# Attention and maxout feed-forward: the feed-forward matmuls cut into 64x64 tiles, in pairs of row halves, with single score units among them

## The chip, the cores and the metric

One core of a Trainium2 chip. The time is device microseconds of one execution; the figure for a kernel is the median of its runs. Profile lines give microseconds from the span's start, and "ns" where they say so. TensorE (PE; its weight loads are PEld), VectorE (DVE), ScalarE (ACT), GpSimd (POOL) and SyncE (SP, which only issues transfers here) each work through their own instruction list in order and wait for one another by semaphores.

## The reference

```python
# q, k, v: 8 batches, 12 heads, 448 positions, 64 wide
scores = scale * np.matmul(q, k.transpose(0, 1, 3, 2))
m = np.max(scores, axis=-1, keepdims=True)
e = np.exp(scores - m)
attn = e / (np.sum(e, axis=-1, keepdims=True) + np.exp(-m) + 1e-09)
x = np.matmul(attn, v)              # then (batch, position, head * 64): 3584 x 768
h = np.maximum(np.maximum(x @ w1, x @ w2), x @ w3)      # w1, w2, w3: 768 x 768
out = h @ w_out                                         # w_out: 768 x 768, out 3584 x 768
```

## The kernel before, in words

Everything that TensorE reads is half precision; PSUM sums are single precision. The order of all work is written out by hand: each engine runs its instructions in the order in which the kernel's functions issue them.

**Attention.** Four heads of a batch form a group, so there are 24 groups, three to a batch (`groups`). For each group k, q and v are loaded by GpSimd's queue (`load_group`, L103) and q and k are transposed. For groups 1 to 6 TensorE does that (`pe_transpose_both`, L172, up to the constant `PE_TR` = 7, L542), 28 transposes and two VectorE copies a group; from group 7 on VectorE reorders q and k (`copy_qk`, L158) and SyncE's queue issues a transposing DMA (`dma_transpose`, L212). Scores are made in *units*: seven key blocks `j` of 64 keys, each four 64x64 matmuls of 448 columns, one on each quarter of the array (`score_tile`, L228; `TILES`, L221, gives row half `r` and column half `c`). The matmuls of row half `r` write PSUM bank `r` of a pair of banks. ScalarE takes the exponential of a unit (L253), VectorE sums the units (`sum_e`, L257). When a group's units are done, `den_group` (L283) makes the column sums of the exponentials with four 64x64 matmuls, and ScalarE turns them into reciprocals by a logarithm and an exponential (`recip_group`, L298); `av_group` (L305) multiplies the exponentials with v, 28 64x64 matmuls into two banks, and VectorE writes the products with the reciprocals into `xT` of the batch (L321).

**Feed-forward.** It is cut into *pieces*. An up piece (`up_piece`, L425) makes 128 hidden features by 448 tokens for one of the three weights: six full 128x128 matmuls of 448 columns into one bank, which VectorE copies or maximizes into `hT`. There are 18 for a batch. (`up_part`, L443, is a smaller form for the first batch.) An output piece (`out_piece`, L469) makes 128 tokens by 384 output features: six full matmuls of 384 columns; VectorE scales the result into `o_sb`, and SyncE's queue writes it out. There are 6 for a batch of even number and 8 for one of odd number (`add_out`).

**The order around the change.** Groups 0 to 3 follow a list of operations (`start`, L566 and on). From group 4 on a loop goes over *visits*: three score units in a row, in some visits with the transposes of a later group, the `av` of one group and the `den` of the next; between two visits `moe` (L526) takes pieces from a list until it has spent a given number of columns (`gap`), and after each piece it issues one waiting VectorE sum (`jobs`). So TensorE goes from full tiles to 64x64 tiles and back once for each visit. When a batch's third `av` is done, its pieces are added to the list.

**PSUM.** Eight banks: two single ones (`single`), taken in turn by pieces and `av`, and three pairs (`double`), taken in turn by score units, `den` and the pieces next to wide visits.

Of the kernel before, what the change touches and what calls it, by code (L numbers as in the profile page):

```python
# [10 lines left out]
FP32 = mybir.dt.float32  # L11
# [11 lines left out]
def kernel(  # L23
# [40 lines left out]
    small = ctx.enter_context(tc.tile_pool(name="small", bufs=2))  # L64
    xt_pool = ctx.enter_context(tc.tile_pool(name="xt", bufs=2))
    ht_pool = ctx.enter_context(tc.tile_pool(name="ht", bufs=2))
    out_pool = ctx.enter_context(tc.tile_pool(name="outp", bufs=3))


    ps1 = ctx.enter_context(tc.tile_pool(name="ps1", bufs=2, space=bass.MemoryType.PSUM))  # L70
    ps2 = ctx.enter_context(tc.tile_pool(name="ps2", bufs=1, space=bass.MemoryType.PSUM))
    turn = [0]

    ctx.enter_context(tc.manual_schedule())

# [3 lines left out]

    def double(name, shape=(512,), dtype=FP32):  # L80
        turn[0] += 1
        return ps2.tile([128, 2, *shape], dtype, tag=f"pair{turn[0] % 3}", name=name)

    groups = [(b, g) for b in range(B) for g in range(NG)]
    raw = {}
# [72 lines left out]
    def copy_qk(i, n):  # L158
# [4 lines left out]
            out=st["qk16"][:, n].rearrange("p j s d -> p s j d"), in_=raw[i]["kq"[n]]  # L163
        )

    def transpose_slots(out, src):
        for s in range(2):
            nc.tensor.transpose(
                out=out[s * KC : s * KC + KC], in_=src[:, s], identity=ident16
            )  # L170

    def pe_transpose_both(i, in_pair=0):  # L172
        st = state.setdefault(i, {})
        st["qkT"] = att_pool.tile([128, 2, NJ, 128], MMDT, tag="qkT", name="qkT")
        if in_pair:
            pair = double("trT", (8, 128), MMDT)
            trT = [pair[:, n, 0:NJ] for n in range(2)]
        else:
            trT = [single("trT", (NJ, 128), MMDT) for n in range(2)]
        for n in range(2):  # L180
            for j in range(NJ):
                transpose_slots(trT[n][:, j, :], raw[i]["kq"[n]][:, :, j])
        for n in range(2):
            nc.vector.tensor_copy(
                out=st["qkT"][:, n].rearrange("p j c -> p (j c)"),
                in_=trT[n].rearrange("p j c -> p (j c)"),
            )


    def first_group():  # L190
# [27 lines left out]
        )  # L218


    TILES = ((0, 0), (0, 1), (1, 0), (1, 1))  # L221
    QK_HALF = {(0, 0): 0, (0, 1): 1, (1, 0): 1, (1, 1): 0}
    V_SLOT = {(0, 0): 0, (0, 1): 1, (1, 0): 1, (1, 1): 0}

    def half(n):
        return slice(n * KC, n * KC + KC)

    def score_tile(qkT, out, j, q0, q1):  # L228
        for r, c in TILES:
# [72 lines left out]
            out=st["rb"], in_=st.pop("lnd"), func=AF.Exp, bias=math.log(LAMBDA), scale=-1.0  # L302
        )

    def av_group(i):  # L305
        b, g = groups[i]
        st = state.pop(i)
        eT, v16 = st["eT"], raw[i].pop("v")
        if g == 0:
            new_x(b)  # L310
        banks = [single("av") for _ in range(2)]
        for j in range(NJ):
            av_tiles(
                [t[:, 0:S] for t in banks],
                lambda r, c: v16[half(r), V_SLOT[r, c], j],
                lambda r, c: eT[half(r), j, c],
                j == 0,
                j == NJ - 1,
            )
        for r in range(2):  # L320
            nc.vector.tensor_tensor(  # L321
                out=xT[b][:, 2 * g + r, :], in0=banks[r][:, 0:S], in1=st["rb"][:, r], op=ALU.mult
            )


    PARTS = ((0, 3), (3, NJ))
# [95 lines left out]
    hT = {}  # L422
    outs = {}

    def up_piece(b, fc, i, bank=None):  # L425
        if b % 2 == 0 and fc == 0 and i == 0:
            hT[b // 2] = ht_pool.tile([128, NFC, 2 * S], MMDT, tag="hT", name="hT")
        dst = hT[b // 2][:, fc, (b % 2) * S : (b % 2) * S + S]
        p_i = single("p_i") if bank is None else bank
        for dc in range(NDC):  # L430
            nc.tensor.matmul(  # L431
                out=p_i[:, 0:S],
                lhsT=w_sb[i][:, dc, ts(fc, 128)],
                rhs=xT[b][:, dc, :],
                start=(dc == 0),
                stop=(dc == NDC - 1),
            )
        if i == 0:
            nc.vector.tensor_copy(out=dst, in_=p_i[:, 0:S])  # L439
        else:  # L440
            nc.vector.tensor_tensor(out=dst, in0=dst, in1=p_i[:, 0:S], op=ALU.max)  # L441
# [24 lines left out]
    NW = DM // NH  # L466
    NT = 2 * S // 128

    def out_piece(bp, t, nh, bank=None):  # L469
        if nh == 0:  # L470
            outs[0] = out_pool.tile([128, DM], FP32, tag="o_sb", name="o_sb")
        o_sb = outs[0]
        op_ps = single("op_ps") if bank is None else bank
        for fc in range(NFC):
            nc.tensor.matmul(  # L475
                out=op_ps[:, 0:NW],
                lhsT=hT[bp][:, fc, ts(t, 128)],
                rhs=wout_sb[:, fc, ts(nh, NW)],
                start=(fc == 0),
                stop=(fc == NFC - 1),  # L480
            )
        last = bp == B // 2 - 1 and t == NT - 1
        cut = nh * NW + (NW // 2 if last and nh == NH - 1 else NW)
        nc.vector.tensor_scalar(  # L484
            out=o_sb[:, nh * NW : cut],
            in0=op_ps[:, 0 : cut - nh * NW],
            scalar1=1.0 / LAMBDA,
            scalar2=None,
            op0=ALU.mult,
        )  # L490
        if cut < nh * NW + NW:
            nc.scalar.activation(  # L492
                out=o_sb[:, cut:DM], in_=op_ps[:, NW // 2 : NW], func=AF.Copy, scale=1.0 / LAMBDA
            )
        if last or nh == NH - 1:
            cols = ts(nh, NW) if last else slice(0, DM)
            for n in range(2):
                b, j = divmod(2 * t + n, NJ)
                b += 2 * bp
                rows = out[b * S : (b + 1) * S].rearrange("(p j) m -> j p m", j=NJ)  # L500
                eng = nc.scalar if last and n == 1 else nc.sync
                eng.dma_start(out=rows[j][:, cols], in_=o_sb[half(n), cols])

    pieces = []

    def add_out(b):
        for t in range(0, 3) if b % 2 == 0 else range(3, 7):
            for nh in range(NH):
                pieces.append((out_piece, (b // 2, t, nh), NFC * (NW + 6)))

    def add_pieces(b):
        for fc in range(NFC):
            for i in range(3):
                pieces.append((up_piece, (b, fc, i), NDC * (S + 6)))
        add_out(b)

    credit = [0.0]
    jobs = []

    def flush():  # L520
        while jobs:
            f, a = jobs.pop(0)
            f(*a)


    def moe(cols, first_in_pair=False, last_in_pair=False):  # L526
# [7 lines left out]
        for n, (f, a, w) in enumerate(run):  # L534
            in_pair = (first_in_pair and n == 0) or (last_in_pair and n == len(run) - 1)
            f(*a, bank=double("piece")[:, 0] if in_pair else None)
            if jobs:
                f, a = jobs.pop(0)
                f(*a)

    NI = len(groups)
    PE_TR = 7  # L542

    load_weight(0, 0, 256)
    load_weight(0, 256, DFF)
# [8 lines left out]
        load_group(i, "v")  # L554
        load_group(i + 1, "kq")

    def add_parts(b, i, part):
        for fp in range(NFC // 2):
            pieces.append((up_part, (b, fp, i, part), 1.0))

    for i, part in ((0, 0), (1, 0), (0, 1), (1, 1), (2, 0), (2, 1)):
        add_parts(0, i, part)
    def sums(i, *units):
        for j in units:
            jobs.append((sum_e, (i, j)))
# [18 lines left out]
    """  # L584
    for op in start.split():
        ops[op[0]](*(int(n) for n in op[1:]))
    credit[0] = 0.0
    for i in range(NG):
        state.pop(i)
    pieces[:] = [  # L590
        (f, a, 2 * NDC * ((PARTS[a[3]][1] - PARTS[a[3]][0]) * KC + 6)) for f, a, w in pieces
    ]
    add_out(0)

    units = [(i, j) for i in range(NG + 1, NI) for j in range(NJ)]
    visits = []
    done = NG
    while units or done < NI:  # L600
        now, units = units[:3], units[3:]
        turned = [i + 1 for i, j in now if j == 3 and i + 1 < PE_TR]
        num = None
        if len(visits) >= 1 and (not turned or done == NG) and (not now or done < now[0][0]):
            num = done
            done += 1
        visits.append((now, turned, num))
    visits.append(([], [], NI))

    gap = sum(w for f, a, w in pieces) / 7.5  # L610
    for n, (now, turned, num) in enumerate(visits):
        for i, j in now:
            if j == 0:
                if i + 2 < NI:
                    load_group(i + 2, "v")
                if i + 3 < NI:
                    load_group(i + 3, "kq")
        wide = num is not None or bool(turned)
        visit(now[:2] if wide else now)
        for i in turned:  # L620
            pe_transpose_both(i)
        if num is not None:
            if num > NG:
                b, g = groups[num - 1]
                av_group(num - 1)
                if g == NG - 1:
                    add_pieces(b)
                    gap = sum(w for f, a, w in pieces) / 7
        if wide:
            visit(now[2:])  # L630
        if num is not None:
            if num < NI:
                den_group(num)
                recip_group(num)
        for i, j in now:
            if j > 0:
                sums(i, j)
            if j == 4 and PE_TR <= i + 2 < NI:
                for n_ in range(2):
                    copy_qk(i + 2, n_)  # L640
                dma_transpose(i + 2)
        last = n == len(visits) - 1
        wide_next = not last and bool(visits[n + 1][1] or visits[n + 1][2] is not None)
        moe(float("inf") if last else gap, wide, wide_next)
        flush()


# [28 lines left out]
```

## Time and profile before

| | before |
|---|---|
| median of 13 runs | 333.74 us (332.55 to 338.3) |
| the profiled execution | 335.65 us |
| its span, first to last instruction | 333.8 us |
| granted TensorE clock, mean | 0.993 |
| TensorE matmuls | 3,281, busy 318.7 us |
| VectorE busy | 236.4 us (71%) |
| ScalarE busy | 188.4 us (56%) |
| DMA traffic | 41.47 MB, mean 124 GB/s |

The span is one execution under the profiler; the runs behind the median are others. The chain of waits that ended last gives TensorE 76% of the span, DMA 15% and the rest to the others; the DMA share lies in the first 65 us. Matmuls overlap in the pipeline, so the mean duration of one (353 ns for 448 columns) is longer than the distance from one start to the next, and only the latter tells the pace.

### The profile page before, as it was taken

What the parts mean: (1) busy time and instruction counts of PE and PEld (TensorE: products, weight loads), DVE (VectorE), ACT (ScalarE), POOL (GpSimd) and SP (SyncE); (2) the same over time, 40 slices, a digit from 0 to 9 for tenths busy, and PEclk for the clock granted to TensorE, in tenths of its full rate; (3) what the DMA queues carried; (4) which work ended last, traced back from release to release, by engine and by line L of the source; (5) the groups of instructions that cost most, each with busy time, mean ns of one, the idle gap of its engine ahead of it and who ended that gap; (6) DMA issues with size and microseconds to landing.
All of it is one profiled execution on the core that took longest, in us unless ns stands there. A gap on an engine that the chain in (4) does not pass through costs nothing.

```text
span 333.8 us, 7919 instructions
## 1 busy us (share of the span) xinstructions
PE 318.7 (95%) x3281; PEld 174.8 (52%) x3281; DVE 236.4 (71%) x443; ACT 188.4 (56%) x227; POOL 101.0 (30%) x172
## 2 busy tenths in 40 slices
PE   6779999899999999999999999999999999999994
PEld 5657676444445545454445545454445545455552
DVE  3446579698877787787868787787878776865552
ACT  2599568697476566666476566657475566410000
POOL 8857549854044041244044032244010000000000
PEclk9799999999999999999999999999999999999999
DMA  8999999999778991989577992989550800013006
GB/s 143 157 190 206 200 193 174 167 205 241 93 82 98 221 188 21 136 137 204 80 90 90 189 197 45 133 150 195 80 84 2 215 32 0 2 47 96 0 11 177
DMA packets 62179, 41.47 MB, mean 124 GB/s; under 512 B 34624, under 2 KB 58688, under 8 KB 62144
## 3 DMA queue, kind: packets, MB, share of 16 engines
q0 software_dynamic: 26208, 21.70, 45.5%
q1 hardware_dynamic: 35632, 18.85, 28.7%
q8 instruction: 25, 0.41, 0.5%
q10 hardware_dynamic: 304, 0.43, 0.5%
q14 instruction: 10, 0.08, 0.1%
HBM read 43.84 MB, written 11.01 MB: 164 GB/s over the span
## 4 chain that ended last, share of the span: by engine, by line
PE 76%; DMA 15%; POOL 3%; DVE 2%; issue 2%; ACT 1%; DVEq 0%; POOLq 0%
PE p_i L431 33%; PE op_ps L475 13%; PE piece L431 11%; PE stp L231 8%; PE av L275 8%; DMA w<-in_moe_w_dram 7%; DMA ld_q<-in_q_dram 3%; DMA w<-in_moe_w_out_dram 3%; PE piece L475 2%; DMA ld_k<-in_k_dram 1%; DVE eS L261 1%; PE den L275 1%; POOL ld_v L98 1%; POOL ld_k L98 1%; POOL ld_q L98 1%
## 5 line engine op out<-in xcount | busy, mean ns | idle before, releaser
L253 ACT ACTIVATE eT<-stp 128x896 f16<-128x896 f32 x147 | 126.2, 916 | 88.5 <-PE stp L231 88.4
L431 PE MATMUL p_i<-xT,w 128*128 128x448 f16 x576 | 114.7, 353 | 0.0
L431 PEld LDWEIGHTS <-w 128*128 128x128 f16 x756 | 71.0, 98 | 75.2 <-issue 12.7
L98 POOL DMA_DIRECT2D ld_v<-in_v_dram x50 | 30.5, 618 | 130.0 <-PE stp L231 125.5
L261 DVE TENSOR_TENSOR eS<-eS,eT 128x896 f16<-128x896 f16 x105 | 64.8, 617 | 0.8
L441 DVE TENSOR_TENSOR hT<-hT,p_i 128x448 f16<-128x448 f16 x69 | 42.9, 621 | 16.7 <-PE p_i L431 16.7
L231 PE MATMUL stp<-qkT 64*64 64x448 f16 (+2 forms) x756 | 49.8, 340 | 3.4 <-DVE hT L463 1.9
L475 PE MATMUL op_ps<-w,hT 128*128 128x384 f16 x270 | 46.9, 327 | 0.0
L475 PEld LDWEIGHTS <-hT 128*128 128x128 f16 x336 | 31.6, 98 | 25.3 <-issue 3.2
L321 DVE TENSOR_TENSOR xT<-av,rb 128x448 f16<-128x448 f32 x42 | 24.3, 619 | 21.5 <-PE av L275 21.5
L431 PE MATMUL piece<-xT,w 128*128 128x448 f16 x180 | 39.1, 353 | 0.0
L98 POOL DMA_DIRECT2D ld_q<-in_q_dram x50 | 30.7, 635 | 6.5 <-DMA w<-in_moe_w_out_dram 1.9
L231 PEld LDWEIGHTS <-qkT 64*64 64x64 f16 x756 | 18.0, 107 | 25.8 <-issue 21.3
L275 PE MATMUL av<-eT,ld_v 64*64 64x448 f16 x588 | 31.5, 349 | 0.0
L484 DVE TENSOR_SCALAR o_sb<-op_ps 128x384 f32<-128x384 f32 (+1 forms) x45 | 24.7, 548 | 7.8 <-PE op_ps L475 7.8
L98 POOL DMA_DIRECT2D ld_k<-in_k_dram x48 | 29.1, 622 | 1.2 <-DMA w<-in_moe_w_dram 1.1
L275 PEld LDWEIGHTS <-ld_v 64*64 64x64 f16 x756 | 21.4, 107 | 11.4 <-issue 1.4
L439 DVE CAST hT<-p_i 128x448 f16<-128x448 f32 x27 | 16.8, 624 | 10.3 <-PE p_i L431 10.3
L340 ACT ACTIVATE eTp<-stp 128x768 f16<-128x768 f32 (+3 forms) x24 | 18.0, 819 | 9.0 <-PE stp L231 9.0
L452 PEld LDWEIGHTS <-w 128*128 128x128 f16 x216 | 18.6, 98 | 5.0 <-issue 3.3
L294 ACT ACTIVATE lnd<-den 128x896 f32<-128x896 f32 x21 | 19.2, 913 | 3.6 <-PE den L275 3.6
L492 ACT ACTIVATE o_sb<-op_ps 128x192 f32<-128x192 f32 x1 | 0.3, 330 | 36.7 <-DVE o_sb L484 36.7
(48 smaller groups left out, 204.7 us busy)
## 6 DMA issues: line engine op xcount, KB each, us to landing
out_dram<-o_sb SPq DMA_DIRECT2D x54, 192.0 KB, 3.1
ld_q<-in_q_dram POOLq DMA_DIRECT2D x50, 112.0 KB, 5.4
ld_v<-in_v_dram POOLq DMA_DIRECT2D x50, 112.0 KB, 4.4
ld_k<-in_k_dram POOLq DMA_DIRECT2D x48, 112.0 KB, 4.9
w<-in_moe_w_dram POOLq DMA_DIRECT2D x6, 192.0 KB, 8.1
w<-in_moe_w_out_dram POOLq DMA_DIRECT2D x3, 384.0 KB, 7.6
w<-in_moe_w_dram POOLq DMA_DIRECT2D x2, 384.0 KB, 7.8
w<-in_moe_w_dram POOLq DMA_DIRECT2D x1, 576.0 KB, 8.9
```

The costliest lines, as they stand in the source:

```text
L98: eng.dma_start(out=dst[hp * KC : hp * KC + KC].rearrange("p s j d -> p s (j d)"), in_=src[:, half_heads(name, hp)],)
L231: nc.tensor.matmul(out=out[half(c), r], lhsT=qkT[half(r), 0, j, h], rhs=qkT[half(r), 1, q0:q1, h], start=True, stop=True,)
L253: nc.scalar.activation(out=st["eT"][:, j], in_=stp[:, :, 0:S], func=AF.Exp, scale=scale, bias=-math.log(EDIV))
L261: nc.vector.tensor_tensor(out=st["eS"], in0=st["eT"][:, 0] if j == 1 else st["eS"], in1=st["eT"][:, j], op=ALU.add,)
L275: nc.tensor.matmul(out=outs[r][half(c)], lhsT=weights(r, c), rhs=moving(r, c), start=start, stop=stop,)
L294: nc.scalar.activation(out=st["lnd"], in_=dps[:, :, 0:S], func=AF.Ln, bias=1.0 / EDIV)
L321: nc.vector.tensor_tensor(out=xT[b][:, 2 * g + r, :], in0=banks[r][:, 0:S], in1=st["rb"][:, r], op=ALU.mult)
L431: nc.tensor.matmul(out=p_i[:, 0:S], lhsT=w_sb[i][:, dc, ts(fc, 128)], rhs=xT[b][:, dc, :], start=(dc == 0), stop=(dc == NDC - 1),)
L441: nc.vector.tensor_tensor(out=dst, in0=dst, in1=p_i[:, 0:S], op=ALU.max)
L452: nc.tensor.matmul(out=p_i[:, ts(j, nq)], lhsT=w_sb[i][:, dc, ts(2 * fp + j, 128)], rhs=xT[b][:, dc, q0 * KC : q1 * KC], start=(dc == 0), ...
L475: nc.tensor.matmul(out=op_ps[:, 0:NW], lhsT=hT[bp][:, fc, ts(t, 128)], rhs=wout_sb[:, fc, ts(nh, NW)], start=(fc == 0), stop=(fc == NFC - 1),)
L484: nc.vector.tensor_scalar(out=o_sb[:, nh * NW : cut], in0=op_ps[:, 0 : cut - nh * NW], scalar1=1.0 / LAMBDA, scalar2=None, op0=ALU.mult,)
```

## The change

The part up to group 6 stays as it is except for three things: `PE_TR` becomes 8, so group 7 too is transposed on TensorE; the transposes of groups 4 to 7 are cut into 64x64 tiles (`transpose_tiles`, 56 small ones a group instead of 28 of 128x64); and two output pieces of the first batch are held back for later.

From group 7, unit 3, on there are no visits. The third pair of PSUM banks is given up, and two single banks take its place, so four single banks turn among the pieces (`ring_bank`) and two pairs among scores, `den` and `av`. A feed-forward piece of six steps is cut twice: each 128x128 matmul becomes four 64x64 ones (row half by column half), and the two row halves of a piece run at different times. A *step* issues the two lower-row matmuls (`r` = 0) of one piece and then the two upper-row matmuls (`r` = 1) of an earlier piece, which trails by `LAG` = 8 half steps and adds to what the lower half left in its bank. An upper half begins with an instruction that waits until the piece's last lower matmuls are done (`wait_for`). Where the next lower half belongs to an output piece, and an up piece of the same hidden block is still in work, the lower half is left out of a step (`idle`).

Score units, `den` and `av` are put singly among the steps, by a table of weights for each group (`ORDER`). `rate` spreads the steps that are left over the three groups of a batch. VectorE's sums and products are issued a given number of steps later (`after`). The last two output pieces of a batch are held until the next batch's up pieces have been listed (`held`). `up_piece` and `out_piece` get a flag, with which they issue the evacuation alone. The output buffers become four.

The core of the diff:

```diff
-    out_pool = ctx.enter_context(tc.tile_pool(name="outp", bufs=3))
+    out_pool = ctx.enter_context(tc.tile_pool(name="outp", bufs=4))
...
+    def transpose_tiles(outs, src):
+        for r, c in TILES:
             nc.tensor.transpose(
-                out=out[s * KC : s * KC + KC], in_=src[:, s], identity=ident16
+                out=outs[r][half(c)], in_=src[half(r), c], identity=ident16[half(r), half(r)]
             )
...
-    PE_TR = 7
+    PE_TR = 8
...
+    HELD = 2
+    held = pieces[-HELD:]
+    del pieces[-HELD:]
...
+    third.close()
+    flush()
+    single_pools.append(ctx.enter_context(tc.tile_pool(name="ps4", bufs=2, space=bass.MemoryType.PSUM)))
+    pair_pools.pop()
+    LAG = 8
...
+    def wait_for(matmuls):
+        nop = nc.tensor.nop()
+        for mm in matmuls:
+            tc.add_manual_dep(
+                nop.ins,
+                mm.ins.name,
+                mybir.DependencyInfo(mybir.DependencyClass.Sync, mybir.DependencyReason.DATA),
+                reason="both row halves write one bank",
+            )
+
+    def half_step(m, k, r):
+        p = flow[m]
+        if r == 0 and k == 0:
+            p["parts"] = piece_parts(p["f"], p["a"])
+            p["bank"] = ring_bank("piece")
+            p["lower"] = []
+        if r == 1 and k == 0:
+            wait_for(p["lower"])
+        w, lhs, rhs = p["parts"]
+        for c in range(2):
+            mm = nc.tensor.matmul(
+                out=p["bank"][half(c), 0:w],
+                lhsT=lhs(k, r, c),
+                rhs=rhs(k, r),
+                start=(r == 0 and k == 0),
+                stop=(r == 1 and k == NDC - 1),
+            )
+            if r == 0 and k == NDC - 1:
+                p["lower"].append(mm)
+        if r == 1 and k == NDC - 1:
+            p["f"](*p["a"], bank=p["bank"], done=True)
...
+    def writers(m, k):
+        return any(p["f"] is up_piece and p["a"][1] == k for p in flow[high[0] // NDC : m])
+
+    def step():
+        if pieces and low[0] == NDC * len(flow):
+            f, a, w = pieces.pop(0)
+            flow.append({"f": f, "a": a})
+        m, k = divmod(low[0], NDC)
+        idle = m == len(flow) or (flow[m]["f"] is out_piece and writers(m, k))
+        if not idle:
+            half_step(m, k, 0)
+            low[0] += 1
+        if high[0] + LAG < low[0] or (idle and high[0] // NDC < low[0] // NDC):
+            half_step(*divmod(high[0], NDC), 1)
+            high[0] += 1
+        steps[0] += 1
+        do_late()
...
+    ORDER = (
+        ("U", 0, 4.5),
+        ("U", 1, 4.5),
+        ("D", 0, 2.2),
+        ("U", 2, 5),
+        ("U", 3, 4),
+        ("N", 0, 2.2),
+        ("U", 4, 8),
+        ("U", 5, 4.5),
+        ("U", 6, 4),
+    )
...
+                visit([(i, j)])
+                steps[0] += 1
+                if j == 2:
+                    recip_group(i - 1)
+                if j > 0:
+                    after({1: 9, 2: 14, 3: 20, 4: 9, 5: 9, 6: 9}[j], sum_e, i, j)
...
+            steps_for(rate[0] * w / TOTAL if i < NI else (8 if op == "D" else 0))
+    while late or left() or high[0] < low[0]:
+        step()
```

## Prediction

> **What bounds the kernel now.** I read the busy rows and the 40 slices first, then the chain of waits in order of time, then the timeline of its two ends.
>
> ```profile
> PE 318.7 (95%) x3281; PEld 174.8 (52%) x3281; DVE 236.4 (71%) x443; ACT 188.4 (56%) x227; POOL 101.0 (30%) x172
> PE   6779999899999999999999999999999999999994
> PEclk9799999999999999999999999999999999999999
> ```
>
> TensorE is busy in every slice from about 80 us on, at the full granted clock, so what counts is how densely its matmuls follow each other. The chain, whose columns are start, length and what (xcount), shows one round:
>
> ```profile
> 118.00 2.27 PE p_i L431 x12
> 120.27 0.69 PE stp L231 x12
> 120.96 3.51 PE p_i L431 x18
> 124.47 0.69 PE stp L231 x12
> 125.16 3.51 PE p_i L431 x18
> ...
> 130.31 1.32 PE av L275 x28
> ```
>
> Twelve feed-forward matmuls take 2.27 us, 0.189 each. Twenty-eight 64x64 matmuls take 1.32 us, again 0.189 per four: four small tiles cost what one full matmul does. But the visit of three score units takes 0.69 instead of 0.567 (+0.12), and the 18 full matmuls after it 3.51 instead of 3.40 (+0.11). So **each stay in 64x64 tiles costs 0.23 us** at its two edges. From 78.25 us, where the second batch's feed-forward starts, to the start of the last matmul at 328.85, I count 41 such stays. The sum agrees: 126 up pieces of 6 x 0.189 = 142.9, 50 output pieces of 6 x 0.163 = 48.9 (0.163 is the plain pace of 384 columns in the timeline), 259 groups of four small tiles x 0.189 = 49.0, together 240.8; the trace has 250.6. The 9.8 left are 41 x 0.23 = 9.4 and small change: nothing else waits there.
>
> The front and the end, by the timeline:
>
> ```profile
> 63.95 0.39 DVE L162 COPY qk<-ld_q 128x896 f16<-128x896 f16 x1 [2.50 <-DMA ld_q<-in_q_dram]
> 65.00 0.38 PE L231 MATMUL stp<-qkT 64*64 64x448 f16 x4 [1.59 <-DVE hT L463]
> 65.43 0.92 ACT L253 ACTIVATE eT<-stp 128x896 f16<-128x896 f32 x1 [1.76 <-PE stp L231]
> ...
> 300.70 20.59 PE L431 MATMUL p_i<-xT,w 128*128 128x448 f16 x108
> 302.04 0.62 DVE L439 CAST hT<-p_i 128x448 f16<-128x448 f32 x1 [0.58 <-PE p_i L431]
> ```
>
> VectorE waits for group 7's q, the evacuation behind that wait comes late, and TensorE and ScalarE stand still 1.6 and 1.8 us. In the last two rows the sixth matmul starts at 300.70 + 5 x 0.189 = 301.65 and its evacuation at 302.04: a result is seen 0.39 us after its last matmul started.
>
> **The change, part by part.**
>
> *Switches.* From group 7 on everything is 64x64, so the 41 stays lose their edges: -9.4 us.
>
> *Pace of the new form.* 1,068 feed-forward steps (126 x 6 + 52 x 6) become four 64x64 matmuls each: two columns on the lower rows for a newer piece, two on the upper rows for an older one, in two banks, as `av` already does. I take the pace of `av`, 0.189, and 0.163 for 384 columns: no change. Two rules of the Trainium skill speak against this.
>
> ```profile
> 20.73 0.36 PE L275 MATMUL den<-eP,ones 64*64 64x192 f16 x8 [1.27 <-DVE eP L358]
> 20.92 0.42 PE L275 MATMUL den<-eTp,ones 64*64 64x192 f16 x12
> 21.17 0.39 PE L231 MATMUL stp<-qkT 64*64 64x256 f16 x8
> 21.39 0.75 PE L275 MATMUL num<-eTp,ld_v 64*64 64x192 f16 x28
> 21.96 0.50 PE L231 MATMUL stp<-qkT 64*64 64x256 f16 x12
> ```
>
> and from the groups of instructions (the columns are count, busy us, mean ns, idle before):
>
> ```profile
> L275 PEld LDWEIGHTS <-ld_v 64*64 64x64 f16 x756 | 21.4, 107 | 11.4 <-issue 1.4
> ```
>
> The skill's "TensorE: Matmul & The Clock Gate", section "Wait — 56ns, not 53.3ns?", gives about 62 ns of sequencer work per matmul where decoding is done in software: four would need 248 ns, 59 more than a step has, +63 us over 1,068 steps. The rows above start just after a 1.27 us wait, when nothing could be queued ahead, and 56 matmuls with 56 loads go out between 20.73 and 21.96: 22 ns per matmul, where the new form needs 47. I take the row. The same page, "The mechanism", says a weight load overlaps running matmuls only in another row group. In the new form each tile's next load meets its own rows busy; a load of 107 ns in the open would give 1,068 x 0.107 = +114 us. In `av` every tile's loads are of that kind, and 28 of them (3.0 us one after another) fit into 1.32 us with no gap. I take the row again: 0.
>
> *Half-empty slots.* An upper half trails its lower half by eight steps. The instruction order shows 8 steps with lower halves only at the start, 8 with upper ones only at the end: 16 half-used slots, so 8 lost x 0.176 (mean of the two paces) = 1.4. At each of seven changes from up pieces to output pieces, the sixth step of the first output piece is held back: three steps of upper halves alone, then three of lower ones, 3 lost x 0.176 x 7 = 3.7. Steps that pair 448 with 384 columns cost up to 13 ns in some 60 places (0.8), and the last lone upper half can run beside the first lone lower one (-0.6); they cancel. +5.1 us.
>
> *Waits.* Every upper half begins with a wait on its own engine, 178 times (126 + 52 pieces). Its signal is due 0.39 us after the lower half's last step; its turn comes three slots later, 0.567 (0.489 in output pieces). Its weight load (0.107) still fits, so: 0. The bound is a load that can't be fetched ahead: the second group of four after a switch starts 24 ns late in the timeline, 178 x 0.024 = 4.3. Queued behind it on TensorE is everything, so a longer wait counts in full.
> Banks: before, a piece's bank is needed again six steps (1.13 us) after its last matmul, and evacuation takes 0.39 + 0.62. Now four banks turn, 10 steps (1.9 us) free: better. Score pairs shrink from three to two; the tightest reuse, unit 1 to unit 2, is 9.7 slots = 1.83 us apart against 0.43 + 0.92. VectorE per group of 12.1 us: six sums at 0.59 start to start, six evacuations at 0.54, 2.3 at 0.47, two products at 0.54, two copies at 0.30 = 9.5 (79%). A sum placed too early can hold an evacuation, so I put 0.8 us here (bounds 0 and 5).
>
> *The front.* Two output pieces move behind the border (2 x 6 x 0.163 = -1.96), one score group moves ahead (+0.19), group 7 is transposed on TensorE instead of by a DMA: 14 groups of four, +1.1 at the 0.081 us of the 192-column `num` groups above (lower bound 0.4), VectorE +2 x 0.54 - 2 x 0.30. The 2.5 us wait for q goes, since group 7's data is wanted two visits later; group 8's copies then stand in their place on VectorE, and SP issues one transpose fewer. By TensorE alone the new section would start at 78.25 - 1.96 + 0.19 + 1.1 - 1.59 - 0.98 (its other two waits there) = 75.0. But ScalarE works without rest there (14 of its 15 us from 65.4 to 80.3); by its work alone only the 1.76 are saved, 76.5. I take **76.0** (bounds 74.4 and 78.3).
>
> *Sum.* 142.9 + 52 x 6 x 0.163 (50.9) + 258 x 0.189 (48.8) = 242.6, + 5.1 + 0.8 = 248.5; from 76.0 the last matmul starts at 324.5 instead of 328.85. The tail (evacuation, last DMA) keeps its 4.95 us. So **-4.35 us**: span 329.45, and the profiled execution 331.3 instead of 335.65. The median of the 13 runs, 333.74, is 0.6% below that execution, so the forecast is 333.74 - 4.35 = 329.4.
>
> **Rivals.**
> 1. *The front's stall goes whole and no wait comes.* The section starts at 74.4 and lasts 247.7: -6.75, so 327.0. For it: 2.6 us of TensorE waits stand there; against it: ScalarE's load. 0.15.
> 2. *Waits take the place of switches.* Single score units are tied to ScalarE and VectorE more closely than visits of three; at the upper bound of 5 us instead of 0.8 the gain is gone: 333.6. Against it: the slack above. 0.11.
> 3. *Slower: the wait ahead of each upper half.* It stands before a weight load, so the sequencer can prefetch nothing past it. It decides from 4.35 / 178 = 24 ns a piece. If the order of releases costs 50 ns (the VectorE-to-TensorE release at 77.9 us took about that), 178 x 0.05 = 8.9, so 338.3. For it: the margin is 0.07 us in up pieces and nearly none in output pieces once the load is counted. Against: the loads can also start late and cost 24 ns at most. 0.21.
> 4. *The change doesn't do what it says*: halves of two pieces don't run side by side, and each takes its own slot: 1,068 more x 0.176 = +188, over 500 us. Against it, `av`'s two rows of tiles, also in two banks, do. 0.03.
>
> **How the numbers follow.** The forecast's own case has 0.50, from 327.9 to 331.5 by the bounds of waits and front. A measurement here tells 0.3% (1 us) from no change. Faster: 0.50 + 0.15 + 0.01 of rival 2 = 0.66; same: 0.10 of rival 2; slower: 0.21 + 0.03 = 0.24. For 8 in 10 the range reaches from 326.3, a little under rival 1, to 337.0, below rival 3's middle: above it lie 0.13 of rival 3 and rival 4, below some 0.03.
>
> **What would show it.** Right: feed-forward groups of four start 0.189 apart (0.163 for outputs) with no wider step at a score unit; lone halves only at the start, the end and seven changes; the first 64x64 feed-forward step near 76 us; the last matmul near 324.5. Wrong: idle TensorE ahead of `piece` released by PE (rival 3), by DVE or ACT around `stp`, `den` (rival 2); a pace above 0.2 in plain stretches; loads of weights in the open.

## The result and the profile after

The changed kernel took **330.14 us** (median of 11 runs, 328.1 to 335.66) where the kernel before took 333.67 (48 runs by now). The ratio is 0.9889, interval 0.9865 to 0.9913: 3.5 us faster by the medians, 3.7 by the ratio. The forecast was 4.35. The ratio compares only executions within 1.5% of the fastest of their kernel; the profiled one (334.75 us, span 332.7) is slower than that, and what slowed it is the most instructive part of this case.

The page of the changed kernel (busy time with instructions, the 40 slices, the queue of instruction blocks with packets, MB and share, and two groups with count, busy us, mean ns and idle before them):

```profile
PE 312.8 (94%) x6625; PEld 250.5 (75%) x6625; DVE 238.4 (72%) x443; ACT 191.8 (58%) x227; POOL 100.4 (30%) x172
...
PE   7779998899977999999999999999999999999994
...
PEclk9799999999997999999999999999999999999998
...
q8 instruction: 52, 0.85, 1.0%
...
L732 PE MATMUL piece<-xT,w 64*64 64x448 f16 x3024 | 177.7, 351 | 1.0 <-issue 1.0
...
L732 PEld LDWEIGHTS <-w 64*64 64x64 f16 x3024 | 127.1, 107 | 22.7 <-issue 1.3
```

TensorE issues twice the instructions in 6 us less busy time. Two things are new. Slices 12 and 13 have a 7 where the kernel before had 9, and the clock falls to 7 in slice 13. And q8, a queue of instruction packets, moved 0.85 MB in 52 packets; the same line of the kernel before is

```profile
q8 instruction: 25, 0.41, 0.5%
```

The rise is TensorE's: 6,688 more matmuls and loads in 0.44 MB are 66 bytes each. A packet has 16,384 bytes in both traces, so it holds about 250 of them.

Away from those slices the new section looks as forecast. The chain of waits of the changed kernel:

```profile
123.07 0.19 PE stp L261 x4
123.26 1.32 PE piece L732 x28
124.58 0.19 PE stp L261 x4
124.77 1.14 PE piece L732 x24
```

A score group lies between feed-forward groups at 0.189, and 28 small feed-forward matmuls take 7 x 0.189. No edge is left. The timeline at the start of the section shows that the halves are less tied than the prediction thought:

```profile
75.17 0.38 PE L261 MATMUL stp<-qkT 64*64 64x448 f16 x4 [0.71 <-ACT eT L283]
75.36 0.95 PE L732 MATMUL piece<-xT,w 64*64 64x448 f16 x8
75.98 1.64 PE L305 MATMUL av<-eT,ld_v 64*64 64x448 f16 x28
```

The section starts at 75.36 (forecast 76.0; before: 78.25). Its first eight matmuls are lower halves alone, four pairs 0.189 apart, so the lower row half is free again at 75.36 + 4 x 0.189 = 76.11. There `av`'s lower half starts, which is issued first; but `av`'s *upper* half, issued behind it, has begun at 75.98: a row half that is free does not wait for the other one's queue. Later, at the last change from up pieces to output pieces, the timeline has both kinds side by side:

```profile
317.12 0.33 PE L732 MATMUL piece<-w,hT 64*64 64x384 f16 x2
317.17 0.35 PE L732 MATMUL piece<-xT,w 64*64 64x448 f16 x2
317.28 0.33 PE L732 MATMUL piece<-w,hT 64*64 64x384 f16 x2
317.36 0.35 PE L732 MATMUL piece<-xT,w 64*64 64x448 f16 x2
317.44 0.33 PE L732 MATMUL piece<-w,hT 64*64 64x384 f16 x2
317.55 0.35 PE L732 MATMUL piece<-xT,w 64*64 64x448 f16 x2
317.61 0.33 PE L732 MATMUL piece<-w,hT 64*64 64x384 f16 x2
317.74 0.35 PE L732 MATMUL piece<-xT,w 64*64 64x448 f16 x2
317.77 0.78 PE L732 MATMUL piece<-w,hT 64*64 64x384 f16 x6
```

Lower output halves follow each other by 0.16 and upper up halves by 0.19, each at its own pace. In the kernel's order of issue the last three upper steps (317.36, 317.55, 317.74) stand alone, and the lower step that starts at 317.28 comes behind all three. So the lone upper steps run beside the lone lower ones that follow them.

And this is slice 12 and 13, in the chain:

```profile
90.11 0.57 PE piece L732 x12
90.68 0.99 issue
91.66 1.52 PE piece L732 x28
...
96.78 1.14 PE piece L732 x24
97.91 4.33 issue
102.25 0.59 PE den L305 x4
102.83 0.75 PE piece L732 x8
```

"Issue" is time in which TensorE waited for nothing that the profile shows. After 4.33 us of it, the next 8 feed-forward matmuls take 0.75 instead of 0.38, the pace of half the clock, until 105 us; the granted clock is 0.50 from 101.6 to 104.9. By the starts of the matmuls the two stops and the slow groups cost 7.0 us.

### The profile page after: what moved, and what is told of

It reads as the page before. It is cut to its first block, busy times and chain, and to the rows that moved or that the text cites. A ratio compares the mean times of both kernels' runs of the same rounds, so it can differ in the third digit from the quotient of the medians.

```text
span 332.7 us, 14614 instructions
## 1 busy us (share of the span) xinstructions
PE 312.8 (94%) x6625; PEld 250.5 (75%) x6625; DVE 238.4 (72%) x443; ACT 191.8 (58%) x227; POOL 100.4 (30%) x172
## 4 chain that ended last, share of the span: by engine, by line
PE 82%; ACT 8%; issue 3%; DVE 2%; POOL 2%; DMA 2%; ACTq 0%; DVEq 0%; POOLq 0%
PE piece L732 58%; PE stp L261 8%; PE av L305 7%; PE p_i L493 4%; ACT eT L283 3%; ACT eTp L377 2%; DMA ld_q<-in_q_dram 2%; PE den L305 1%; PE piece L493 1%; ACT rb L331 1%; POOL ld_q L111 1%; ACT lnd L324 1%; ACT lnd L421 1%; POOL ld_k L111 1%; DVE eS L291 1%
## 5 line engine op out<-in xcount | busy, mean ns | idle before, releaser
L732 PE MATMUL piece<-xT,w 64*64 64x448 f16 x3024 | 177.7, 351 | 1.0 <-issue 1.0
L732 PEld LDWEIGHTS <-w 64*64 64x64 f16 x3024 | 127.1, 107 | 22.7 <-issue 1.3
L482 DVE TENSOR_TENSOR hT<-hT,piece 128x448 f16<-128x448 f16 x84 | 52.0, 619 | 29.5 <-PE piece L732 27.0
L732 PE MATMUL piece<-w,hT 64*64 64x384 f16 x1248 | 71.9, 323 | 0.2
L261 PE MATMUL stp<-qkT 64*64 64x448 f16 (+2 forms) x756 | 68.8, 336 | 2.2 <-ACT eT L283 0.7
L732 PEld LDWEIGHTS <-hT 64*64 64x64 f16 x1248 | 46.3, 107 | 15.6 <-PE piece L732 2.2
L525 DVE TENSOR_SCALAR o_sb<-piece 128x384 f32<-128x384 f32 (+1 forms) x56 | 30.8, 552 | 12.2 <-PE piece L732 11.4
L480 DVE CAST hT<-piece 128x448 f16<-128x448 f32 x42 | 26.1, 622 | 14.2 <-PE piece L732 13.6
L493 PEld LDWEIGHTS <-w 128*128 128x128 f16 x216 | 18.6, 98 | 5.6 <-issue 3.8
L331 ACT ACTIVATE rb<-lnd 128x896 f32<-128x896 f32 x21 | 19.9, 950 | 0.2
```

The source lines that it names most:

```text
L261: nc.tensor.matmul(out=out[half(c), r], lhsT=qkT[half(r), 0, j, h], rhs=qkT[half(r), 1, q0:q1, h], start=True, stop=True,)
L493: nc.tensor.matmul(out=p_i[:, ts(j, nq)], lhsT=w_sb[i][:, dc, ts(2 * fp + j, 128)], rhs=xT[b][:, dc, q0 * KC : q1 * KC], start=(dc == 0), ...
L525: nc.vector.tensor_scalar(out=o_sb[:, nh * NW : cut], in0=op_ps[:, 0 : cut - nh * NW], scalar1=1.0 / LAMBDA, scalar2=None, op0=ALU.mult,)
L732: mm = nc.tensor.matmul(out=p["bank"][half(c), 0:w], lhsT=lhs(k, r, c), rhs=rhs(k, r), start=(r == 0 and k == 0), stop=(r == 1 and k == ND ...
```

## The experiments

**The front alone.** In the kernel before, group 7 too is transposed on TensorE instead of by a DMA.

```diff
-    PE_TR = 7
+    PE_TR = 8
```

> The kernel before with one part of the change alone: group 7, too, is transposed on TensorE. The theory (the gain is the removed switches less the half-empty slots, and about 2 us of the front) expects the VectorE wait of 2.5 us for q near 61 to 64 us and the 1.6 us stand of TensorE behind it to go, against 1.1 us more of transposes: 0 to -1.5 us, so 332.2 to 333.7. The rival (the whole gain comes from the front's waits, and the 64x64 section breaks even) expects -3 to -4 us, about 330.

Measured: 333.58 against 333.68, ratio 1.0008 (0.9982 to 1.0035). No gain. In its profile the sixth group's sum (`den`) comes at 75.8 instead of 77.94, so the stall does go; but the last matmul starts at 327.96, only 0.9 earlier, and a stop of 1.0 us that before did not have stands at 187.7, where `av` waits for VectorE. In this profile most of what the front gains is given back at that wait. This is a part of the changed kernel's front: two output pieces that it moves are not in it.

**More switches.** In the kernel before, every narrow visit of three score units is split in two with one feed-forward piece between: 86 stays in 64x64 tiles instead of 61.

```diff
-        visit(now[:2] if wide else now)
+        visit(now[:2])
+        if not wide and now[2:]:
+            if pieces:
+                f, a, w = pieces.pop(0)
+                credit[0] -= w
+                f(*a)
+            visit(now[2:])
```

> The kernel before, with each visit of three score units and nothing else cut in two and one feed-forward piece put between: 86 stays in 64x64 tiles instead of 61, and the same work. If a stay costs 0.23 us at its edges and nothing hides it, 25 x 0.23 = +5.8 us, about 339.4. If the edges are hidden by the wait for a bank or for ScalarE, or cost more only in the trace's modelled ends, 0 to +1 us.

Measured: 339.25, ratio 1.0179 (1.0133 to 1.0224): 5.6 us more than 333.68, for 25 stays 0.22 each. The chain of its profile:

```profile
82.32 0.50 PE stp L231 x8
82.83 1.24 PE p_i L431 x6
84.07 0.31 PE stp L231 x4
```

Eight small matmuls take 0.50 instead of 0.378, four take 0.31 instead of 0.189: +0.12 whatever their number, and +0.11 behind them (1.24 instead of 1.13). The cost belongs to the stay, as the prediction had it.

**Fewer lone halves.** In the changed kernel an output piece's step is held back whenever any up piece for the same row of `hT` still lacks its upper half. Here only pieces whose tokens it reads count, which leaves 42 fewer lone halves.

```diff
-        return any(p["f"] is up_piece and p["a"][1] == k for p in flow[high[0] // NDC : m])
+        bp, t, nh = flow[m]["a"]
+        read = {2 * bp + (t * 128) // S, 2 * bp + (t * 128 + 127) // S}
+        return any(
+            p["f"] is up_piece and p["a"][1] == k and p["a"][0] in read
+            for p in flow[high[0] // NDC : m]
+        )
```

> The changed kernel, where the lower half of an output piece is held back only for up pieces of the batches whose tokens it reads. The held pieces then never wait, and the order has lone halves only at the start and the end (16 instead of 58). Theory: the seven changes lose 3 steps of 0.176 us each, so -3.1 to -3.7 us less some new waits for hidden values, about 327. Rival (lone halves are no loss, since the other row half's matmuls could not have run faster beside them): 0, about 330.

Measured: 330.0 (327.72 to 331.74), ratio 0.9897 (0.9854 to 0.994). Nothing gained: 42 halves cost nothing that can be measured, as the rival expected.

**A lag of seven steps, and the changed kernel again.** The upper half trails by 7 steps instead of 8, so that its wait on TensorE itself comes two slots after the signal's matmul instead of three.

```diff
-    LAG = 8
+    LAG = 7
```

> The changed kernel with the upper halves seven half steps behind instead of eight, so that an upper half begins two slots (0.378 us, 0.326 in output pieces) after its lower half's last step. If the release takes the 0.39 us that VectorE needs and a weight load can be late at 24 ns, each of 178 pieces loses 0.01 to 0.09 us: +2 to +16 us. If the wait is served within the engine sooner, as matmuls end in order: 0 to -0.2 us (one slot less at each end).

Measured: 332.52 (330.67 to 337.69), ratio 0.9945 (0.991 to 0.9979), 2.4 us above the changed kernel by the medians, 1.9 by the ratios. But plain stretches of its profile have no wait ahead of the upper halves; it has stops of 0.4 and 1.9 us near 84 and 90 us, put down to "issue". So the lag was not cleanly tested here.

> The changed kernel once more, unaltered, as the yardstick for the three kernels beside it on the same chip: 330.1 as before. In its trace, wherever TensorE stops with nothing to wait for, a 16 KB instruction block should have come later than the 6 us that 256 instructions last; stops of another kind (released by VectorE, ScalarE, TensorE) should sum to under 2 us.

The changed kernel, unedited, gave 330.11 (326.78 to 334.31), ratio 0.9867 (0.983 to 0.9904), and its profile has the stops at the same place of the program: 1.36 us at 89.45 and 4.06 us at 97.06. It is no accident of one execution. Its instruction packets came late, as expected: at 79.5, 88.1 and 98.5 us, 8.5 to 11.2 after the one before.

**No loads behind group 9.** To see whether transfers cause the stops, the loads of q, k and v from group 10 on are left out and group 9's data is used in their place; the transposing DMAs, the output's DMAs and all engine work stay.

```diff
+            if i > 9:
+                tiles[name] = kept[name]
+                continue
...
+            if i == 9:
+                kept[name] = tiles[name]
```

> The changed kernel without the loads of q, k and v from group 10 on: those groups use group 9's data again, so their results are not the reference's, and all engines but GpSimd do the same work. Theory (TensorE's instruction blocks, now twice as many, are fetched late where the transfer engines are full, and it stops): the stops between 78 and 105 us shrink or go, and the time falls by the 1 to 3 us that separate typical runs from an undisturbed one: 327 to 329, with less scatter. Rival (the stops come from the new order's waits, or from the clock): no change, 330.

Measured: **326.5** (325.9 to 328.07), ratio 0.9801 (0.9775 to 0.9827), 3.6 us below the changed kernel in the same set of runs by the medians, 2.2 by the ratios, and below the 327 to 329 that the theory expected. The same edit on the version with fewer lone halves:

> As the kernel beside it without late loads (groups from 10 on use group 9's data), with the exact hold-back of output pieces as well. With the disturbance by transfers taken away, the pair tells what the 42 lone halves at the changes from up to output pieces cost. If the two row halves run strictly in the order of issue: -3.1 us against the kernel beside it. If a row half's matmul may start ahead of an earlier one of the other half, as the trace at 75.9 us suggests: 0 to -1.5 us.

326.93 (325.76 to 328.31): again nothing from those halves, now without the disturbance. The long stops are gone in both profiles, and the DMA side shows why. These are stretches of the changed kernel (busy time and instructions of PE, PEld, DVE, ACT and POOL, then granted clock, mean share of the 16 transfer engines, GB/s; a share above 1 means that packets overlap on an engine):

```profile
78.00:90.00 12.00, 12.00 (x257) 11.70 (x254) 10.04 (x19) 7.95 (x9) 4.39 (x8) 1.00 1.50 159
90.00:99.50 9.50, 6.92 (x142) 4.97 (x135) 6.42 (x12) 4.58 (x5) 3.24 (x6) 1.00 1.30 111
99.50:105.00 5.50, 2.75 (x32) 1.78 (x35) 0.62 (x1) 1.91 (x3) 0.00 (x0) 0.69 0.37 60
```

Without the late loads the shares of the first two stretches are 0.23 and 0.08. This is the second one there:

```profile
90.00:99.50 9.50, 9.50 (x208) 9.35 (x202) 7.87 (x15) 7.28 (x9) 0.00 (x0) 1.00 0.08 16
```

The instruction packets of the trace, in time, tell the rest. In quiet parts one starts every 6 us, about every 256 matmuls and loads of TensorE: that is how long a block now lasts, since it takes eight instructions where it took two to fill 0.189 us. In the changed kernel they start at 69.4, 80.3, 89.2 and 99.8. Up to the first stop TensorE has executed 3,251 matmuls and loads, up to the second 3,507: exactly 256 apart, so each stop lies at the end of a block. TensorE goes on 2.5 us after the packet of 89.2 has started, and again 2.4 us after that of 99.8. In quiet parts a packet starts about one block, 6 us, before TensorE needs it; that of 89.2 starts 1.5 us before the stop, and that of 99.8 when TensorE has stood for 1.9 us. Between them no instruction packet moved at all; the queues of the stretch from 90.5 to 99.5 (packets, MB, share of the 16 engines):

```profile
q0 software_dynamic: 729, 0.58, 65.7%
q1 hardware_dynamic: 1826, 0.46, 65.4%
```

q0 carries the loads, q1 the small packets (252 bytes in the mean) of the transposing DMA. In the same stretch the kernel without late loads has two q8 packets. The Trainium skill ("Runtime: NRT & Kernel Launch", section "Instruction fetch mechanics") says that instructions come in blocks of 256, the next fetched while the current one runs, and that crossing a block's end is mostly hidden. The trace agrees with the first; the second fails here, where a block lasts 6 us and its fetch comes 9 to 11 us after the one before. In the kernel before, blocks come 12 to 18 us apart in this part of the program, and none of its stops there is of this kind, under a share of 1.04:

```profile
78.00:90.00 12.00, 12.00 (x82) 5.71 (x83) 9.33 (x18) 7.26 (x9) 3.25 (x6) 1.00 1.04 171
```

**Spread transfers.** If that is the cause, moving the transfers should serve as well as removing them. To the version with fewer lone halves: group 9's transposing DMA goes three units later within group 7, v loads one unit later, q and k loads from the border on at unit 4.

```diff
-            if j == (4 if i < 6 else 2) and PE_TR <= i + 2 < NI:
+            if i < 7 and j == (4 if i < 6 else 2) and PE_TR <= i + 2 < NI:
...
-                if j == 0:
-                    if i + 2 < NI:
-                        load_group(i + 2, "v")
-                    if i + 3 < NI:
-                        load_group(i + 3, "kq")
+                if j == 1 and i + 2 < NI:
+                    load_group(i + 2, "v")
+                if j == 4 and i > MID and i + 3 < NI:
+                    load_group(i + 3, "kq")
...
-                if j == (9 if i == 7 else 3) and PE_TR <= i + 2 < NI:
+                if j == (5 if i == 7 else 3) and PE_TR <= i + 2 < NI:
```

> All of the reference's work: the changed kernel with the exact hold-back, and with its transfers spread: group 9's transposing DMA three score units later, v loads at unit 1 and q and k loads at unit 4 instead of all at unit 0. If late instruction blocks cost 1 to 3 us a run, part of that returns: 328 to 329.5. If the stops have another cause, as the exact hold-back alone: 330.

Measured: **327.57** (326.79 to 327.86), ratio 0.9819 (0.9797 to 0.9841), 2.5 us below the changed kernel beside it by the medians, 1.6 by the ratios, and the best version that does the whole work. Its profile:

```profile
78.00:90.00 12.00, 12.00 (x258) 11.69 (x254) 10.42 (x22) 8.15 (x10) 4.59 (x8) 1.00 1.26 180
90.00:99.50 9.50, 9.50 (x208) 9.35 (x204) 7.88 (x16) 7.04 (x8) 2.08 (x4) 1.00 0.59 82
99.50:105.00 5.50, 5.50 (x131) 5.25 (x125) 5.05 (x10) 2.66 (x3) 3.56 (x6) 1.00 1.01 160
```

It moves more bytes in the first stretch (180 GB/s against 159) at a lower share, TensorE doesn't stop in these stretches, and its instruction packets start at 78.9, 86.6, 90.6, 95.6 and 102.2. Two short "issue" stops are left later, 0.14 and 0.20 us at 124.7 and 189.5, each behind a packet that came 10 us after the one before.

**The lag again, undisturbed.** The spread version with a lag of 6 and of 7.

> The kernel with spread transfers and exact hold-back, upper halves six half steps behind: an upper half starts one slot (0.189, 0.163 us) after its lower half's last step. If TensorE learns of its own result after 0.39 us as VectorE does, each of 178 pieces waits about 0.2 us and everything behind it too: +36 us, about 363. If the engine keeps the order by itself and the signal costs nothing: 327.

> The same with seven half steps: two slots, 0.378 and 0.326 us. By a release of 0.39 us: 0.01 us in 126 pieces and 0.06 in 52, +4.4 us, 332. If the plain stretches stay without a wait, as the earlier kernel with seven showed outside the changes: 327 to 328.

Lag 7: 327.9 (327.49 to 328.79), ratio 0.9836 (0.9804 to 0.9868), 0.3 above lag 8 and within the scatter. Lag 6: **340.51** (340.04 to 340.69), ratio 1.0206 (1.017 to 1.0242), 12.9 above it: 72 ns for each of 178 pieces, neither of the two expectations. Its timeline:

```profile
140.53 0.33 PE L732 MATMUL piece<-w,hT 64*64 64x384 f16 x2
140.77 0.11 PEld L732 LDWEIGHTS <-w 64*64 64x64 f16 x2 [0.31 <-PE piece L732]
140.77 0.38 PE L732 MATMUL piece<-xT,w 64*64 64x448 f16 x2
...
140.78 0.51 PE L732 MATMUL piece<-w,hT 64*64 64x384 f16 x4
...
140.98 0.35 PE L732 MATMUL piece<-xT,w 64*64 64x448 f16 x2
```

The weight load of the up piece's first upper step waits for TensorE itself. In this trace 163 loads of the feed-forward do so, at lag 7 none. The signal is that of the up piece's last lower step, which started at 140.34; the semaphore moves at 140.73 and the load starts at 140.77. So TensorE sees its own signal 0.42 us after the matmul's start, no sooner than VectorE's 0.39. By that, one slot (0.189) would cost 0.23 us a piece. It costs less because the row halves need not keep step: here the upper half has fallen a whole slot behind, and its first step starts together with the next lower one (140.77 and 140.78). Two slots, 0.378, are still short of 0.42, and what is missing shows as 0.24 instead of 0.19 ahead of the upper half; the step after it takes 0.21.

At lag 7 the nominal distance is two slots, also under 0.42, and yet nothing waits. One piece in that trace: the last lower step starts at 82.25, its second matmul, which signals, at 82.28, the semaphore moves at 82.64, the load starts at 82.68 and the upper half at 82.71. Upper steps start at 82.33, 82.52 and 82.71, lower ones at 82.25, 82.43 and 82.62, so each half keeps its 0.189 and the upper one runs 0.08 us behind. That shift isn't paid again at each piece.

**Added traffic.** To the spread version and to the kernel before, a useless second load of k for groups 10 to 21.

```diff
+        if "k" in which and 10 <= i < 22:
+            spare = ld_pool.tile([128, 2, NJ, D], MMDT, tag="ld_x", name="ld_x", bufs=2)
+            for hp in range(2):
+                load_half(nc.gpsimd, spare, "k", i, hp)
```

> The kernel with spread transfers and eight half steps, plus useless traffic: k of groups 10 to 21 is loaded a second time into a tile that nothing reads. Theory (instruction blocks of 6 us come late when the transfer engines are full): stops of TensorE with nothing to wait for, +1 to +5 us. If late blocks are not the cause of the stops: 0.

> The kernel before with the same useless traffic. Its blocks of 256 instructions last about 12 us in the same section, so by the theory a late block does no harm: within 1 us of 333.5. If the traffic delays the work itself (loads of k and q), it hurts here as much as in the kernel beside it.

Measured: the spread version 329.82 (327.1 to 334.02), ratio 0.9863 (0.9808 to 0.9918), 2.2 us more than without by the medians, but the intervals of the two ratios overlap; the kernel before 336.8 (334.86 to 338.2), ratio 1.0098 (1.0062 to 1.0134), 3 us more. The second missed its expectation. The kernel before suffers too, but by late data, as the timeline of its profile shows:

```profile
85.18 0.57 PE L235 MATMUL stp<-qkT 64*64 64x448 f16 x8 [1.50 <-DMA qkT<-qk]
...
113.38 0.56 DVE L488 TENSOR_SCALAR o_sb<-op_ps 128x384 f32<-128x384 f32 x1 [1.72 <-DMA out_dram<-o_sb]
```

So the times of this pair don't tell late instructions from late data. The profiles do in part: the spread version with added traffic has an "issue" stop of 0.41 us at 95.4 that it lacks without, and the kernel before with added traffic has none in this part of the program.

**All "issue" stops together.** The traces of these runs allow one more count. In the 64x64 section, six profiles have stops of TensorE of over 0.05 us put down to "issue": the changed kernel (both times), the first lag 7, fewer lone halves, spread transfers, and spread with added traffic. There are 11, and counted in matmuls and loads they lie at five places: 2,995, 3,251, 3,507, 4,787 and 7,603, all whole multiples of 256 apart. The section, from its first feed-forward step to the start of the last matmul, lasts 245.2 to 252.8 us in the seven profiles with a lag of 8. Less these stops, and less the slow groups after the long one, it lasts 245.2 to 245.5 in all seven, with the loads or without. So these stops account for what those profiles differ by in the section.

## Why the prediction came out right

The sign and the mechanism of the gain hold. That the size came out is in part luck: two terms of the sum were wrong, one mis-sized and one missing, and they cancelled. The last matmul, forecast at 324.5, starts at 327.8 in the profile with the long stops and at 320.7 in that of the version with fewer lone halves, which has hardly any.

**Switches (-9.4): right.** 0.22 to 0.23 per stay by the added switches, and none left in the changed kernel's plain stretches.

**Pace of the new form (0): right.** Feed-forward groups start 0.189 and 0.163 apart. Of the two rules weighed against it neither decides here: in plain stretches a matmul and its load go out every 47 ns, and loads into row halves that are busy stay hidden.

**Half-empty slots (+5.1): the mis-sized step.** The prediction took a slot with one row half in use as a slot lost, because it counted slots in the order of issue; only the last lone upper half was let run beside a lower one (-0.6). The row halves keep their own order: a half's next matmul starts as soon as its half is free, past earlier ones of the other half. Lone halves of one kind are then made up by lone halves of the other. Without the late loads the section runs from 74.65 to 319.94, 245.3 us, where the plain sum is 242.6: half-empty slots *and* waits come to 2.7 instead of 5.9. About 0.7 of it are three stops of over 0.26 us between starts, so at most 2.0 is left for the slots. Removing 42 lone halves changed nothing, twice. Two of the three stops stand at changes to output pieces (283.3 and 309.9; in the changed kernel the latter is at 317.77). There the lower half has run ahead: its last step starts at 309.41, but its signal comes only at 310.28, just behind that of the upper step at 309.87, which was issued before it. So a lower half that runs ahead still reports in the order of issue, and the next upper half waits for that.

**Waits (0.8): right; rival 2 did not come.** The section without late loads has little room for more, as just summed.

**The wait ahead of each upper half (0; rival 3): right at a lag of 8, with more margin than thought.** The 0.39 us taken for the signal was nearly right (0.42 to the next weight load). The margin comes from the row halves again, which may shift by up to a slot against each other without loss. Rival 3 is real two steps further: at a lag of 6 the kernel is slower than before, by the 72 ns per piece that the prediction's own threshold of 24 ns would call decisive.

**The front (76.0): near, but its worth isn't shown.** Section starts are 75.36 in the changed kernel and 74.2 in the spread one. The transposes of group 7 took 0.48 us (56 matmuls from 64.16 to 64.64), not 1.1: the lower bound of 0.4 was nearer. In the kernel before, the part that could be tried alone gained nothing. The profiled execution of before was also 1.9 us above its median, so a sum against it can count waits that most executions don't have.

**The term that was missing.** Nothing in the prediction costs instruction delivery; its part on the sequencer asked how fast instructions leave it, not how they reach it. By medians, the change is worth 6.9 us without the late loads (333.41 to 326.5) and 3.3 with them, in the same runs: 3.6 us are lost there (2.2 by the ratios), and 2.5 of them (1.6) come back when the transfers are spread. That took away what the slots had spared, and the forecast of 4.35 fell between.

**The rivals.** Rival 1's time of 327.0 is nearly what the spread version gives, though by the slots and not by the front's stall. Rival 4 is refuted by the pace.

**What stays open.** That the stops are late instruction blocks is shown by their places (256 apart) and their packets. That the blocks were late because the transfer engines were full is supported by the versions with loads removed and with loads moved, and by the one stop that added traffic brought back, not by the times with added traffic, which rose in both kernels. Which of the transfers holds the packets up, the loads or the small packets of the transposing DMA, was not separated. The first lag 7 run was slower than the lag alone explains. In its one profile the block-end stops cost 2.6 us, and the section without them lasts some 1.3 us longer than at lag 8: it has five stops of about 0.26 us released by TensorE itself, where lag 8 has two. With the exact hold-back they are gone.

## What to carry to other kernels

A stay in another tile size costs at its two edges whatever its length, so count the stays, not the matmuls in them; putting all of a section in the small size takes the cost away if the small form keeps the pace. Small tiles also multiply an engine's instructions: check how long a block of them lasts against the gaps between the packets of the instruction queue, above all where the transfers' share is above 1 (1.3 to 1.5 around the long stops here), and where "issue" stops appear, move transfers before touching the matmuls. When counting lost slots, count each row half of the array by itself, and let the halves shift against each other before you charge a wait to every piece.

## What the hardware did that was not expected

- Row halves of 64x64 tiles run out of the order of issue: `av`'s upper half began at 75.98, ahead of its lower half, issued before it, at 76.11; at the last change to output pieces a lower step started at 317.28, ahead of upper ones issued before it at 317.36, 317.55 and 317.74.
- Their signals stay in the order of issue: without the late loads, a lower step of 309.41 reported at 310.28, behind the upper step of 309.87.
- TensorE ran dry of instructions for 0.99 and 4.33 us with nothing to wait for, at ends of blocks of 256 matmuls and loads; after the longer stop groups of four took 0.37 instead of 0.19, with the granted clock at 0.50 from 101.6 to 104.9.
- A signal from TensorE to itself is seen 0.42 us after its matmul's start, about as late as VectorE sees one (0.39).
